# Four of the later token tiles normalised on GpSimd instead of VectorE, in the prologue of an adaLN block

## The chip, the cores and the metric

The kernel runs on one core of one Trainium2 chip. The core's engines work side by side, each through its own list of instructions in order: TensorE (PE in the profile, with its weight loads as PEld), VectorE (DVE), ScalarE (ACT), GpSimd (POOL) and SyncE (SP), which issues nearly all DMAs. They wait for each other through semaphores. The metric is the time of one execution on the device in microseconds (us), as the median of several runs. The span of a profiled execution is from its first to its last instruction.

## The reference

One transformer block whose two halves are modulated by a condition vector `c`. There are 2048 tokens of width 1024, 32 query heads of width 32 that share one key and one value head, and a gated feed-forward part of width 3584. Everything is stored as bf16.

```python
mod = (silu(c) @ w_mod).reshape(1, 6, 1, 1024)
sa, ca, ga, sb, cb, gb = mod[:, 0], ..., mod[:, 5]
h = layernorm(x) * (1 + ca) + sa
q = (h @ wq) split into 32 heads of 32;  k = h @ wk;  v = h @ wv
o = softmax(q k^T / sqrt(32)) v          # k and v are shared by all heads
x = x + ga * (o @ wo)
h = layernorm(x) * (1 + cb) + sb
x = x + gb * ((silu(h @ w1) * (h @ w3)) @ w2)
```

## The kernel before

**Tiling.** Tokens come in 16 tiles of 128. A tile lies in `X` with tokens on partitions. It is normalised there, written to a scratch tile (`XN` and other regions that are free at that time), transposed by TensorE in 128x128 pieces and stored in `HT`, with channels on partitions. Keys `KT` (four copies, one for each quarter of the partitions), values `V` and queries `QT` are projected from `HT`. Attention runs over 8 blocks of 256 queries. In a block, the heads come in 8 groups `f` of four. A step of attention (function `step`) takes one group and 256 keys: eight score matmuls (line 915) into two of three pairs of PSUM banks, then two exponentials on ScalarE (line 925). A whole block has 64 steps, and the kernel 512, with 1024 exponentials. Sums of exponentials on VectorE (lines 942 to 957), products with `V` (line 975) and with a selection matrix for the softmax denominators (line 1002) follow, and their results are taken from PSUM by VectorE (lines 1011 to 1028). After each block, `post` adds the output projection (line 1107), normalises again and computes the feed-forward part (lines 1141 and 1175), while the next block's exponentials run.

**Prologue.** Before the first scores, the scale and shift of the first modulation are computed from `w_mod`, the first eight token tiles are normalised and transposed, and the keys of the first 1024 tokens are projected. The scale is folded into the weights, the shift into biases (function `bias`; its matmuls are on line 758). The first block treats the groups f = 0 to 3 specially: it first takes all four over the first half of the keys, then all four over the second half. So the exponentials begin while tiles 8 to 15 are still to be normalised, transposed and turned into keys and values. The norm of a tile has these steps, in functions `ln`, `ln_stats`, `ln_scale` and `ln_norm`:

- two statistics instructions on VectorE (line 530) and one that joins them (line 532);
- on GpSimd, adding epsilon (line 551) and the power -0.5 (line 553), which give the reciprocal standard deviation `RS`;
- one `tensor_scalar` over 128x1024 elements (line 573), which subtracts the mean and multiplies by `RS`. It runs on the engine that `en` names, here VectorE for all 16 tiles. Tiles 2 and 5 have their statistics on ScalarE.

Four normalised tiles are transposed together (function `tr`, matmuls on line 587) in four groups of eight matmuls, two channel chunks each; VectorE takes tiles 8 to 15 out of PSUM (line 601, two instructions for each group).

**PSUM banks.** There are eight. During attention six belong to the scores. What else TensorE does in the prologue from 29 us on goes through the two others, `PB[0]` and `PB[1]`: the bias products, the projections of keys, values and queries (lines 637, 648 and 658), the transposes of tiles 8 to 15, and the products of line 975 and 1002. A bank is free when its result has been taken out.

**The order of the work.** No engine's list is written out by hand. `Dag.add` collects the instructions with what they read and write, an engine, a priority (smaller is earlier) and a cost in us; `Dag.schedule` plays the execution through with these costs and fixes for each engine the order in which it will run; `Dag.emit` writes the lists and the semaphores. The costs only set the order. The rules that matter here:

- TensorE takes a score step that is ready first. Then come transposes and key projections (priority 1) and the bias products (priority 0). Value and denominator products come before query projections (priority 5) while TensorE is in the mode of scores and value products, or when they have been ready for more than 1 us; otherwise after them.
- A group of matmuls that opens a bank is placed only when a bank is free. Query, key and value projections open their banks in the order of the program: q of f=2, q of f=3, then the keys of the second half.
- VectorE takes the smallest priority, and of equal ones the earlier in the program; what has been ready for more than 4 us is raised by 3. Evictions have 1 or less, statistics and norms 2.
- GpSimd takes norms (priority 2) before the small steps of the reciprocal standard deviation (priority 5).

The cost of a norm in this planning is in `ln_norm`:

```python
writes=[("XN", q)] + xnk(q), dur=0.42 if en == "dve" else 1.2, prio=2 - bp)
```

The prologue's token tiles go through

```python
def ln(t):
    (ln_stats_act if t in ONACT else ln_stats)(t)
    ln_scale(t, 1)
    ln_norm(t, t, en="pool" if t in ONPOOL else "dve")
```

The norms inside `post` call `ln_norm` without `en` and run on VectorE.

Of the kernel before, what the change touches and what calls it, by code (L numbers as in the profile page):

```python
# [380 lines left out]
def build(nc, x_in, wq_in, wk_in, wv_in, wo_in, w1_in, w3_in, w2_in, c_in, wmod_in, out, S, D, F):  # L381
# [167 lines left out]
    def ln_scale(t0, n):  # L549
        rk = [("RS", t0 + i) for i in range(n)]  # L550
        G.add("pool", lambda e: e.tensor_scalar(RS[:, t0:t0 + n], MV[:, t0:t0 + n, 1], EPS, None, ALU.add),
              reads=[("MV", t0 + i) for i in range(n)], writes=rk, dur=0.3)
        G.add("pool", lambda e: e.tensor_tensor(RS[:, t0:t0 + n], RS[:, t0:t0 + n], NHALF[:, 0:n], ALU.pow),
              reads=rk + ["NHALF"], writes=rk, dur=0.4)
# [16 lines left out]
    def ln_norm(t, q, s=None, bp=0, en="dve"):  # L571
        s = t % NXS if s is None else s
        G.add(en, lambda e: e.tensor_scalar(xnt(q), X[:, s, :], MV[:, t, 0:1], RS[:, t:t + 1],
                                               ALU.subtract, ALU.mult),
              reads=[("X", s), ("RS", t), ("MV", t)], writes=[("XN", q)] + xnk(q), dur=0.42 if en == "dve" else 1.2, prio=2 - bp)
# [90 lines left out]
        return [("QT", f, q0 + i) for i in range(0, qn, P)]  # L666

    ONACT = (2, 5)
    ONPOOL = ()
    KP = 1  # L670
    QACT = 1
    TRP = 1
# [5 lines left out]
# [5 lines that stand above are left out]
# [549 lines left out]
def bass_adaLN_cond__grouped_kv_mqa__glu_gated_swiglu__prompt_kernel(nc, A_x, A_wq, A_wk, A_wv, A_wo, B_x, B_w1, B_w3, B_w2, c, w_mod, out):  # L1232
    _, S, D = [int(v) for v in A_x.shape]
    F = int(B_w1.shape[1])
    build(nc, A_x, A_wq, A_wk, A_wv, A_wo, B_w1, B_w3, B_w2, c, w_mod, out, S=S, D=D, F=F)
# [28 lines left out]
```

## Time and profile before

| what | us |
|---|---|
| median of 3 runs (1159.92 to 1161.35) | 1159.93 |
| the profiled execution, its whole time | 1159.92 |
| its span | 1158.1 |
| busy: TensorE, ScalarE, VectorE, GpSimd | 1122.6, 1027.6, 984.7, 43.5 |
| 1024 exponentials on ScalarE (line 925) | 968.6 |
| norms of tiles 8 to 15 on VectorE, mean of one | 0.53 to 0.54 |
| ScalarE idle between 30 and 62 us, four waits before exponentials (2.56, 0.76, 1.29, 5.57) | 10.2 |

The mean granted clock of TensorE was 0.990. How to read the rows: a row of the timeline has the start, the length of the stretch, engine, line, operation, what it writes and reads with the shape, and how many instructions were joined (`x8`); in brackets stand the idle time of the engine before it and what ended it. A row of a group has the busy time of all its instructions and the mean of one in ns. `WREG`, `GSB`, `GBB` and `UREG` as outputs of line 573 are scratch for normalised tiles: 8 to 13 go to `WREG`, 14 to `GSB`, 15 to `GBB`. The six banks of the scores are called `SP` in the rows and the other two `PB`.

### The profile page before, as it was taken

The numbers are of one execution on the slowest core, as the hardware profiler recorded it, in microseconds if no ns is written. First come the engines' busy times: TensorE is split into PE (matmuls) and PEld (weight loads), VectorE is DVE, ScalarE is ACT, GpSimd is POOL, SyncE is SP. The second block draws the span as 40 slices with busy tenths as digits, with TensorE's granted clock in tenths as the row PEclk, the third lists the DMA queues.
The fourth block names the chain that finished last, engine by engine and source line by source line (L and its number), as shares of the span: only waits on it lengthen the run. The fifth ranks groups of instructions, "written<-read, shape, count | busy, mean of one in ns | idle before, by whom it ended". The sixth has DMA issues, their size and how long they took to land.

```text
span 1158.1 us, 35702 instructions
## 1 busy us (share of the span) xinstructions
PE 1122.6 (97%) x15918; PEld 767.1 (66%) x15918; DVE 984.7 (85%) x1498; ACT 1027.6 (89%) x1170; POOL 43.5 (4%) x86
## 2 busy tenths in 40 slices
PE   7799998999979999999999999999999999999998
PEld 6564444776646766777577766776677766777887
DVE  5837889999888999899999998999989999997452
ACT  5789999999999999999999999999999999992110
POOL 3200001000000001000100001000100010000000
PEclk8899999999989999999999999999999999999999
DMA  9337005956546565856496567766586649756996
GB/s 331 113 129 220 19 2 127 275 169 178 166 122 190 169 193 149 248 170 192 119 279 196 159 177 194 226 169 174 152 252 181 185 122 258 204 152 192 284 291 160
DMA packets 385417, 211.10 MB, mean 182 GB/s; under 512 B 21744, under 2 KB 376048, under 8 KB 385264
## 3 DMA queue, kind: packets, MB, share of 16 engines
q1 hardware_dynamic: 383184, 208.69, 64.5%
q8 instruction: 125, 2.05, 0.8%
q10 hardware_dynamic: 2080, 0.13, 0.1%
q14 instruction: 28, 0.23, 0.1%
HBM read 201.46 MB, written 4.19 MB: 178 GB/s over the span
## 4 chain that ended last, share of the span: by engine, by line
PE 92%; ACT 3%; DVE 3%; DMA 1%; SPq 1%; issue 0%; POOL 0%; DVEq 0%
PE PB L1141 33%; PE PB L1175 16%; PE SP L915 14%; PE PB L975 11%; PE PB L1107 5%; PE PB L658 4%; PE SP L1141 3%; ACT UREG L925 3%; PE SP L1175 2%; PE PB L1002 2%; DMA UREG<-in_w_mod_dram 1%; PE PB L637 1%; PE PB L838 0%; PE SP L1107 0%; DVE WO L850 0%
## 5 line engine op out<-in xcount | busy, mean ns | idle before, releaser
L925 ACT ACTIVATE UREG<-SP 128x1024 bf16<-128x1024 f32 x1024 | 968.6, 1075 | 18.8 <-PE SP L915 16.4
L948 DVE TENSOR_TENSOR UREG<-UREG 128x2048 bf16<-128x2048 bf16 x240 | 292.8, 1220 | 12.8 <-ACT UREG L925 10.8
L915 PE MATMUL SP<-QT,KT 32*128 32x256 bf16 x4096 | 204.8, 274 | 16.0 <-ACT UREG L925 15.0
L1141 PE MATMUL PB<-QT,WREG 128*128 128x256 bf16 x1648 | 207.4, 274 | 1.8 <-DVE DSB L1026 1.6
L1141 PEld LDWEIGHTS PB<-QT,WREG 128*128 128x128 bf16 x1648 | 150.1, 98 | 46.8 <-issue 31.2
L942 DVE TENSOR_TENSOR UREG<-UREG 128x2048 bf16<-128x2048 bf16 x120 | 146.4, 1220 | 11.5 <-PE PB L1002 6.4
L915 PEld LDWEIGHTS SP<-QT,KT 32*128 32x128 bf16 x4096 | 61.2, 93 | 138.6 <-ACT UREG L925 79.6
L1141 PE MATMUL PB<-QT,HREG 128*128 128x256 bf16 x1056 | 133.7, 274 | 0.8 <-DVE DSB L1026 0.8
L975 PE MATMUL PB<-UREG,V 128*32 128x256 bf16 x4032 | 132.2, 277 | 1.7 <-DVE QT L610 0.9
L975 PEld LDWEIGHTS PB<-UREG,V 128*32 128x32 bf16 x4032 | 99.3, 98 | 27.5 <-issue 17.9
L1141 PEld LDWEIGHTS PB<-QT,HREG 128*128 128x128 bf16 x1056 | 96.1, 98 | 29.7 <-issue 19.6
L1175 PE MATMUL PB<-WREG,HREG 128*128 128x256 bf16 x812 | 101.2, 273 | 0.0
L1175 PEld LDWEIGHTS PB<-WREG,HREG 128*128 128x128 bf16 x812 | 75.3, 98 | 20.4 <-issue 11.4
L1175 PE MATMUL PB<-HREG 128*128 128x256 bf16 x532 | 67.8, 274 | 0.0
L1141 PE MATMUL PB<-QT,X 128*128 128x256 bf16 x528 | 67.8, 274 | 0.0
L658 PE MATMUL PB<-HREG,WREG 128*128 128x512 bf16 (+1 forms) x312 | 64.1, 343 | 0.3 <-DVE DSB L1026 0.3
L957 DVE TENSOR_TENSOR UREG<-UREG 128x2048 bf16<-128x2048 bf16 x52 | 63.4, 1220 | 0.5
L1150 ACT ACTIVATE GSB<-GSB 128x512 bf16<-128x512 bf16 x56 | 38.8, 693 | 27.5 <-DVE GSB L1148 27.5
L1014 DVE COPY XN<-PB 128x256 f32<-128x256 f32 x63 | 26.6, 422 | 39.6 <-PE PB L1002 39.3
L1175 PEld LDWEIGHTS PB<-HREG 128*128 128x128 bf16 x532 | 49.2, 98 | 14.3 <-issue 8.0
L1107 PE MATMUL PB<-WO,QT 128*128 128x512 bf16 x232 | 57.6, 381 | 0.2 <-DVE QT L661 0.2
L1141 PEld LDWEIGHTS PB<-QT,X 128*128 128x128 bf16 x528 | 48.2, 98 | 14.3 <-issue 9.3
(139 smaller groups left out, 1031.9 us busy)
## 6 DMA issues: line engine op xcount, KB each, us to landing
WREG<-in_B_w_dram SPq DMA_DIRECT2D x112, 512.0 KB, 5.1
HREG<-in_B_w_dram SPq DMA_DIRECT2D x74, 512.0 KB, 5.2
WREG<-in_B_w_dram SPq DMA_DIRECT2D x33, 896.0 KB, 5.1
X<-in_B_w_dram SPq DMA_DIRECT2D x38, 512.0 KB, 5.1
HREG<-in_B_w_dram SPq DMA_DIRECT2D x21, 896.0 KB, 5.2
X<-in_B_w_dram SPq DMA_DIRECT2D x10, 896.0 KB, 5.1
X<-in_A_x_dram SPq DMA_DIRECT2D x32, 256.0 KB, 5.0
WREG<-in_w_mod_dram SPq DMA_DIRECT2D x16, 512.0 KB, 4.7
```

The lines of the kernel that those rows point to most:

```text
L658: g = mm_group(NC, lambda e, b, c: e.matmul(b[:, 0:n], WQ[:, c, f * P:(f + 1) * P], HT[:, c, sl], start=c == 0, stop=c == NC - 1), lambda ...
L915: r = e.matmul(SP[:, b, o:o + qn], KT[32 * gg:32 * gg + 32, kts[j] * P:(kts[j] + 1) * P], QT[32 * gg:32 * gg + 32, f, q0:q0 + qn], start=T ...
L925: G.add("act", lambda e, u=u, h0=h0, n=n, b0=b0, nb=nb: e.activation(U[:, u, h0 * W:(h0 + n) * W].rearrange("p (b w) -> p b w", b=nb), SP[ ...
L942: G.add("dve", lambda e, tr=tr, u=u, fu=first_u: e.tensor_tensor(TR[:, tr, 0:4 * W], U[:, fu, 0:4 * W], U[:, u, 0:4 * W], ALU.add), reads= ...
L948: G.add("dve", lambda e, tr=tr, u=u: e.tensor_tensor(TR[:, tr, 0:4 * W], TR[:, tr, 0:4 * W], U[:, u, 0:4 * W], ALU.add), reads=[("TR", tr) ...
L957: G.add("dve", lambda e, ta=ta, tb=tb: e.tensor_tensor(TR[:, ta, 0:4 * W], TR[:, ta, 0:4 * W], TR[:, tb, 0:4 * W], ALU.add), reads=[("TR", ...
L975: r = e.matmul(PB[g.bank][32 * gg:32 * gg + 32, 0:qn], V[:, kt, :], U[:, pu, (gg * npk + j) * qn:(gg * npk + j + 1) * qn], start=w0 + n == ...
L1014: G.add("dve", lambda e, g=g, f=f: e.tensor_copy(ASB[:, f % 4, 0:qn], PB[g.bank][:, 0:qn]), writes=[("ASB", f % 4), ("XN", 2 + f % 4 // 2) ...
L1107: g = mm_group(NC, lambda e, b, f, t=t, h=h: e.matmul(b, QT[:, f, t * P:(t + 1) * P], WO[:, f, h * 512:(h + 1) * 512], start=f == 0, stop= ...
L1141: return e.matmul(b[:, j * qn:(j + 1) * qn], w13[:, w, c, j * P:(j + 1) * P], QT[:, c, q0:q0 + qn], start=c == 0, stop=c == NC - 1)
L1150: G.add("act", lambda e, b=b: e.activation(TB[b], GS[b], ACT.Tanh, scale=0.5), reads=[("GS", b)], writes=[("TB", b)], clear=alias("TB") if ...
L1175: G.add("pe", lambda e, g=g, j=j, fc=fc, hf=hf, first=first, w2s=w2s: e.matmul(PB[g.bank][:, j * 256:(j + 1) * 256], HHT[:, hf * NH + fc, ...
```

## The change

The tuple that names the token tiles whose norm runs on GpSimd was empty and now holds four tiles.

```diff
     ONACT = (2, 5)
-    ONPOOL = ()
+    ONPOOL = (9, 11, 13, 15)
     KP = 1
```

For tiles 9, 11, 13 and 15, `ln` now calls `ln_norm` with `en="pool"`: the same `tensor_scalar` of 128x1024 elements, with the same operands, is put on GpSimd's list, with a planning cost of 1.2 in place of 0.42. The statistics of these tiles stay on VectorE, and tiles 8, 10, 12 and 14 are normalised on VectorE as before. As every list comes from the planner, the order of other instructions can change too.

## The prediction

> **What bounds the kernel now.** I read the table of busy time by stage first, then ScalarE's, TensorE's and VectorE's instructions in order of time between 26 and 62 us, then GpSimd's rows. Columns of the stage table: length, busy us of TensorE (PE), its weight loads (PEld), VectorE (DVE), ScalarE (ACT) and GpSimd (POOL), each with a count, then the granted clock and DMA.
>
> ```profile
> core 0: us, PE busy (x) PEld busy (x) DVE busy (x) ACT busy (x) POOL busy (x), PEclk, DMA share, GB/s
> 35.00:47.00 12.00, 9.79 (x217) 6.28 (x216) 10.31 (x27) 9.38 (x10) 4.08 (x10) 0.72 0.33 90
> 47.00:62.00 15.00, 12.16 (x262) 8.62 (x265) 11.99 (x36) 9.41 (x11) 0.99 (x2) 1.00 0.44 121
> 62.00:90.00 28.00, 27.68 (x523) 18.69 (x516) 10.07 (x22) 27.42 (x30) 0.00 (x0) 1.00 0.31 108
> 400.00:600.00 200.00, 199.19 (x2864) 134.64 (x2861) 185.06 (x273) 198.98 (x224) 6.86 (x8) 1.00 0.68 188
> 1100.00:1158.00 58.00, 53.70 (x492) 47.84 (x490) 22.69 (x35) 5.66 (x9) 0.00 (x0) 1.00 0.90 226
> ```
>
> From 62 us ScalarE and TensorE are both full (27.4 and 27.7 of 28; 199.0 and 199.2 of 200), and after the last exponential (1047 us) TensorE alone works off the rest. So time is still to be had where both stand idle, at the start, and what ScalarE gains before 62 us should reach the end. The norms that the change moves run from 34.9 to 51.3 us, in two stages in which PE lacks 2.2 and 2.8 us and ACT 2.6 and 5.6 us.
>
> ```profile
> 35.60 7.44 ACT L925 ACTIVATE UREG<-SP 128x1024 bf16<-128x1024 f32 x8 [2.56 <-PE SP L915]
> 43.80 1.94 ACT L925 ACTIVATE UREG<-SP 128x1024 bf16<-128x1024 f32 x2 [0.76 <-PE SP L915]
> 47.02 9.27 ACT L925 ACTIVATE UREG<-SP 128x1024 bf16<-128x1024 f32 x10 [1.29 <-PE SP L915]
> 61.86 19.00 ACT L925 ACTIVATE UREG<-SP 128x1024 bf16<-128x1024 f32 x20 [5.57 <-PE SP L915]
> ```
>
> In brackets is the idle time before a row. The four waits of the exponentials are the region's cost. The longest, 5.57 us, is for the first scores of head group f=3, whose queries are projected only after all transposes:
>
> ```profile
> 40.90 1.00 PE L758 MATMUL PB<-SAB,WO 128*128 128x1 bf16 x32
> 48.52 1.07 PE L587 MATMUL PB<-IDENT,WREG 128*128 128x128 bf16 x16
> 55.40 0.40 PE L587 MATMUL PB<-IDENT,WREG 128*128 128x128 bf16 x4 [0.40 <-DVE HREG L601]
> 59.67 1.05 PE L658 MATMUL PB<-HREG,WREG 128*128 128x256 bf16 x8
> 61.41 0.40 PE L915 MATMUL SP<-QT,KT 32*128 32x256 bf16 x8
> ```
>
> Transposes (48.5 to 55.9), two value and denominator products (56.1 to 59.7), the projection, then the scores: one line through the two free PSUM banks PB0 and PB1, emptied by VectorE.
>
> **The change part by part.**
>
> *VectorE.* Four norms leave it. Each takes 0.534 us, 0.46 from start to start, so 1.8 us in all; those of tiles 9, 11 and 13 (39.95, 42.80, 44.56) stand in a gapless stretch, that of 15 (50.73) amid the transposes' evictions. No DMA is added; X slots 1, 3, 5 and 7 are handed on by GpSimd instead, and the loads behind them (35.5 on) are first needed after 170 us: nothing.
>
> *GpSimd.* The trace has no such instruction. Nearest rows:
>
> ```profile
> L521 POOL COPY QT<-SCT 128x512 bf16<-128x512 bf16 x2 | 1.2, 611 | 4.1 <-DVE SCT L518 4.1
> ```
>
> ```profile
> 185.60 1.08 POOL L551 TENSOR_SCALAR RS<-MV 128x1 f32<-128x1 f32 x1 [135.42 <-DVE MV L532]
> 186.77 0.57 POOL L553 TENSOR_TENSOR RS<-RS,NHALF 128x1 f32<-128x1 f32 x1
> ```
>
> Half the columns take 0.61, so 0.61 is the lower end and 1.22 the doubled row. The same L551 takes 0.21 where VectorE is in its statistics and 1.08 here, beside a 1.17 us VectorE add that ends with it: GpSimd was held. Two such holds of 0.9 give 3.0, the upper end. I take 1.22, plus 0.3 for one hold. What stands behind each on GpSimd is the rstd pair (0.22 + 0.57) of the next tiles, and VectorE waits for those in order.
>
> On this the Trainium skill (SBUF — State Buffer, Who interferes with whom) speaks against the change: one port pair is shared, a VectorE tensor_scalar in its fast mode and any GpSimd instruction exclude each other, and whichever comes second is blocked for the whole of the other. The row agrees for GpSimd as the one held; no row shows VectorE held. By the rule each moved norm could cost VectorE a whole GpSimd norm where one of its own falls on it, an estimated 4 x 1.2 = 4.8 us, and the sum would turn from 2.4 us gained to 2.4 lost.
>
> I add no such loss: beside the places that I work out for the four norms below, VectorE's list has statistics and PSUM evictions, and one norm.
>
> *Order.* The list is planned with 1.2 us for a GpSimd norm (0.42 on VectorE). I worked the planner's rules through from 39.95; they decide order, the times are this trace's.
> 1. Without tile 9's norm the two v evictions (L651) start 0.45 earlier, bank PB1 frees, and the bias product L758, which stood behind the score step of 40.34, is put before it. At half clock (0.50 granted from 39.0 to 45.6) it runs 40.3 to 41.25. The scores land at 41.8 instead of 40.95: new wait of ScalarE, 41.9 - 41.17 = 0.7.
> 2. TensorE is now in score mode when PB0 frees, and in that mode the planner takes the value and denominator products of f=0 (1.83 + 1.74 at half clock) before q of f=2. They end at 45.3, the next scores at 45.7: ScalarE waits from 43.75, 2.0, where it waited 0.76 + 1.29.
> 3. By then tiles 8 to 11 are normalised (tile 11 on GpSimd: 42.6 to 43.8), so the transposes go next: TensorE 45.8 to 49.35, set by evictions at 0.36 and the norms of 12 and 14. VectorE reaches tile 15's last statistics only at 49.6, so when a bank frees there the second four aren't ready, and q of f=2 goes in at 49.6. Evicted at 51.15, it gives scores at 51.7: ScalarE, done at 49.5, waits 2.4.
> 4. Norm 15 on GpSimd: 49.65 + 0.85 (rstd) + 1.2 = 51.7; TensorE comes for it at 52.6. The second transposes run under the eight exponentials of f=2 (51.85 + 8 x 0.927 = 59.3), and so does q of f=3, evicted at 57.4. It is wanted at 58.35. The wait of 5.57 goes.
> 5. Late next are the second half's keys: at 61.2 by this order, first needed after f=3 at 66.7.
>
> Sum: away 0.76 + 1.29 + 5.57 = 7.62; new 0.7 + 2.0 + 2.4 = 5.1; gain 2.5 us. ScalarE enters the full stretch at 59.3 instead of 61.86. TensorE then stands 0.4 us of products behind where it stood; it has 2.6 us of idle from 90 to 120 and 12.5 from 120 to 400 to take them. I keep 2.4.
>
> The profiled execution took 1159.92 us, span 1158.1 and 1.8 around it, as the median 1159.93. Predicted: 1159.9 - 2.4 = 1157.5.
>
> *A longer norm.* With duration p, tile 15 is ready at max(49.65, 44.5 + 2p) + 0.85 + p. TensorE is late from p = 2.1, ScalarE (0.95 in hand) from 2.7; at 3.0 the gain shrinks to 1.6 (54.35 - 52.6 - 0.95 = 0.8 lost), and at 3.5 it is gone. Below 1.22 nothing is gained, as VectorE's queue, not GpSimd, brings tile 15's statistics.
>
> **The rivals.** 0.2%, or 2.3 us, is about what a measurement of this kernel can tell from no change.
>
> *A shorter queue, same order.* The transposes stay behind the scores of f=2. Then VectorE's 0.6 us of statistics at 47.04 leaves the path to q of f=2, and 0.46 goes between evictions; the transposes end 1.1 sooner and so do q and scores of f=3: 1158.8. For it: ScalarE's stretch from 47.02 is full and sets those score steps. Against: the bias product's weights are issued at 23.4 and land within 10.5, by 33.9, so that it lacks only the bank.
>
> *Slower: both queries behind all eight transposes.* If tile 15 is normalised before the bank frees at 49.6, the transposes keep both banks to 52.5; then value products to 54.3, q of f=2 at 55.3, scores at 55.9. ScalarE waits 7.0 from 49.5, the two groups end at 56.4 + 14.8 = 71.2 instead of 61.86 + 7.4 = 69.3: 1.9 later, 1161.8, and up to 2 more if so long a gap halves the granted clock again, as it was after the thin stretch before 39 us. It decides if tile 15 is normalised 2.1 us sooner than I have it; its aggregate stands behind six evictions and two norms on VectorE, which the planner's priorities put first.
>
> *More.* TensorE's later idle shrinks too, since the keys of the second half and value products are done sooner against the scores: up to 1.5 of the 2.6 us from 90 to 120, so 1156.0.
>
> *GpSimd is slow.* At p = 4.5 tile 15 is ready at 58.85, 6.2 late, and scores of f=3 come 2.7 later than now: 1162.6. The rows speak against it: it needs more than three holds for each norm.
>
> That the norms stay on VectorE is excluded: ln passes the engine by tile, and all four tiles go through it.
>
> **How the numbers follow.** My forecast 0.48 (own range 1156.4 to 1158.8), more 0.15, same order 0.17, slower by order or clock 0.15, slow GpSimd 0.05. The forecast lies on the bound, so 0.29 of its 0.48 count as faster. Faster: 0.29 + 0.15 + 0.02 of the shorter queue = 0.46; slower: 0.12 of the order's 0.15 and the 0.05 = 0.17; the rest, 0.37, within 0.2%. The order is replanned to the end of the kernel, where I followed it only to 62 us; ScalarE is idle some 8 us from there to 1047, so little can be won and some lost. Range 1154.8 to 1162.3.
>
> **What would show it.** The bias product ahead of a score step near 40 us; transposes of tiles 8 to 11 at about 46 instead of 48.5; q of f=2 between the two sets of transposes; scores of f=3 right behind those of f=2, with no wait over 3 us on ScalarE after 50 us; GpSimd norms of 1.2 to 1.5 us; VectorE norms that stay at 0.53. Wrong if the norms take over 2.6 us, if VectorE is held, if the granted clock halves between 47 and 56, or if ScalarE's waits after 62 us grow by what was won.

## The result and the profile after

The changed kernel takes 1166.41 us (median of 4 runs, 1164.16 to 1167.61) against 1159.93 us. The ratio is 1.0051, with a 95% interval of 1.0033 to 1.0070: slower by 4 to 8 us, where 2.4 us less was predicted and the range ended at 1162.3. The profiled execution took 1167.1 us, with a span of 1165.3 us. TensorE's time in that span went from 1122.6 us busy and 35.5 idle to 1125.4 busy and 39.9 idle; more idle time and slower matmuls both count.

The table of busy time by stage, changed kernel, with the columns of the table shown before:

```profile
core 0: us, PE busy (x) PEld busy (x) DVE busy (x) ACT busy (x) POOL busy (x), PEclk, DMA share, GB/s
35.00:47.00 12.00, 9.66 (x210) 6.42 (x208) 11.03 (x26) 8.68 (x10) 10.24 (x10) 0.72 0.25 68
47.00:62.00 15.00, 8.48 (x108) 5.74 (x112) 7.56 (x22) 8.67 (x10) 9.72 (x7) 0.68 0.33 88
62.00:90.00 28.00, 27.57 (x570) 18.63 (x566) 11.61 (x28) 24.08 (x26) 0.00 (x0) 0.99 0.41 134
110.00:116.00 6.00, 4.60 (x60) 1.97 (x57) 6.00 (x15) 5.16 (x7) 0.00 (x0) 0.82 0.93 284
52.40:62.60 10.20, 5.54 (x64) 4.00 (x68) 5.45 (x16) 4.17 (x6) 4.41 (x2) 0.50 0.38 103
```

The stage from 47 to 62 us carries the damage. TensorE is busy for 8.5 of its 15 us, where it had 12.2, the granted clock is 0.68 instead of 1.00 (0.50 from 52.4 to 62.6 us), and GpSimd, which had 1 us of work there, has 9.7. From 110 to 116 us the clock is 0.82, where before it was 1.00. GpSimd's instructions in order of time show what fills it:

```profile
35.54 3.81 POOL L573 TENSOR_SCALAR WREG<-X,MV,RS 128x1024 bf16<-128x1024 bf16 x1 [2.10 <-DVE WREG L573]
...
43.17 3.80 POOL L573 TENSOR_SCALAR WREG<-X,MV,RS 128x1024 bf16<-128x1024 bf16 x1
46.93 0.56 POOL L553 TENSOR_TENSOR RS<-RS,NHALF 128x1 f32<-128x1 f32 x1
47.47 0.22 POOL L551 TENSOR_SCALAR RS<-MV 128x1 f32<-128x1 f32 x1
47.68 3.80 POOL L573 TENSOR_SCALAR WREG<-X,MV,RS 128x1024 bf16<-128x1024 bf16 x1
51.45 0.55 POOL L553 TENSOR_TENSOR RS<-RS,NHALF 128x1 f32<-128x1 f32 x1
...
53.11 3.80 POOL L573 TENSOR_SCALAR GBB<-X,MV,RS 128x1024 bf16<-128x1024 bf16 x1
```

A norm on GpSimd takes 3.80 us, seven times VectorE's 0.54. The small steps of the reciprocal standard deviations (551 and 553) stand between the norms: the second step of tile 14 waits from 47.69 until norm 13 has ended, and tile 15's own pair comes after that. So tile 15 is ready at 56.91. TensorE in that stretch:

```profile
45.74 1.05 PE L658 MATMUL PB<-HREG,WREG 128*128 128x256 bf16 x8
...
51.01 0.40 PE L915 MATMUL SP<-QT,KT 32*128 32x256 bf16 x8 [0.66 <-ACT UREG L925]
57.06 0.58 PE L587 MATMUL PB<-IDENT,WREG 128*128 128x128 bf16 x4 [5.65 <-POOL GBB L573]
...
58.85 0.61 PE L915 MATMUL SP<-QT,KT 32*128 32x256 bf16 x8
...
61.88 1.39 PE L975 MATMUL PB<-UREG,V 128*32 128x256 bf16 x32
...
64.07 1.05 PE L658 MATMUL PB<-HREG,WREG 128*128 128x256 bf16 x8
```

It waits 5.65 us for norm 15. Behind that wait, in the order of the list, stand not only the transposes of tiles 12 to 15 but a score step of f=2 (58.85), then the value and denominator products, and the queries of f=3 (64.07). The exponentials show this as two waits:

```profile
41.91 1.94 ACT L925 ACTIVATE UREG<-SP 128x1024 bf16<-128x1024 f32 x2 [0.76 <-PE SP L915]
45.86 1.94 ACT L925 ACTIVATE UREG<-SP 128x1024 bf16<-128x1024 f32 x2 [2.01 <-PE SP L915]
48.10 5.61 ACT L925 ACTIVATE UREG<-SP 128x1024 bf16<-128x1024 f32 x6 [0.30 <-PE SP L915]
59.52 1.94 ACT L925 ACTIVATE UREG<-SP 128x1024 bf16<-128x1024 f32 x2 [5.81 <-PE SP L915]
...
66.26 3.89 ACT L925 ACTIVATE UREG<-SP 128x1024 bf16<-128x1024 f32 x4 [2.65 <-PE SP L915]
```

ScalarE waits 5.81 us in the middle of f=2 and 2.65 before f=3, which starts at 66.26 instead of 61.86: 4.4 us later. From the starts of the later exponentials in both traces, 1.1 us is added by 79 us and 2.8 between 104 and 124 us, 1.3 of it comes back, and from 352 us to the last exponential the distance is constant at 7.2 us, which is also that of the spans (1165.3 - 1158.1).

### The profile page after: what moved, and what is told of

It is laid out like the page before. It is cut to its first block, busy times and chain, and to the rows that moved or that the text cites. A ratio compares the mean times of both kernels' runs of the same rounds, so it can differ in the third digit from the quotient of the medians.

```text
span 1165.3 us, 35683 instructions
## 1 busy us (share of the span) xinstructions
PE 1125.4 (97%) x15908; PEld 766.6 (66%) x15908; DVE 985.1 (85%) x1494; ACT 1028.4 (88%) x1170; POOL 58.3 (5%) x90
## 4 chain that ended last, share of the span: by engine, by line
PE 91%; DVE 3%; ACT 2%; POOL 1%; DMA 1%; SPq 1%; issue 1%; DVEq 0%
PE PB L1141 33%; PE PB L1175 16%; PE SP L915 14%; PE PB L975 10%; PE PB L658 5%; PE PB L1107 4%; PE SP L1141 3%; PE SP L1175 2%; PE PB L1002 2%; ACT UREG L925 2%; SPq L695 1%; DMA UREG<-in_w_mod_dram 1%; DVE ST L530 1%; PE PB L637 1%; PE PB L838 0%
## 5 line engine op out<-in xcount | busy, mean ns | idle before, releaser
L551 POOL TENSOR_SCALAR RS<-MV 128x1 f32<-128x1 f32 x32 | 19.3, 609 | 1008.4 <-DVE MV L532 1008.3
```

## The experiments

Two theories stood at the outset. A: the length of the GpSimd norms is the cause, through what stands behind them on GpSimd and TensorE, and the new order by itself gains. B: the new order of the lists is the cause, whatever engine runs the norms. Ratios below are to the kernel before, run on the same chip beside each kernel.

**Short norms in the new order.** GpSimd's norms treat 320 of the 1024 columns; the rest is set to zero, once, at the start.

```diff
-        G.add(en, lambda e: e.tensor_scalar(xnt(q), X[:, s, :], MV[:, t, 0:1], RS[:, t:t + 1],
+        w = D if en == "dve" else SHORT
+        G.add(en, lambda e: e.tensor_scalar(xnt(q)[:, 0:w], X[:, s, 0:w], MV[:, t, 0:1], RS[:, t:t + 1],
```

> The changed kernel, every list in the same order, but the four GpSimd norms take only the first 320 of their 1024 columns (the other 704 are set to zero at the start and stay zero, so these four tiles are not normalised in full). By 3.80 us for 1024 columns a norm should last about 1.2 us, which is what the planning charged. Theory A, the length of the GpSimd norm is the whole loss: the 5.65 us in which TensorE waited for the norm of tile 15 goes, the first exponentials of f=3 start at 66.3 - 5.8 - 0.3 = 60.2 or earlier, ahead of the 61.9 of before, and the time is 1157.5 to 1159. Theory B, the new order itself loses: the start of f=3 improves likewise, but the 3.5 us that the changed kernel lost after it (exponentials 4.4 us late at f=3, 7.9 us late at step 48) are lost again, and the time is 1161 to 1163. Theory C, sharing between GpSimd and VectorE: VectorE norms beside a GpSimd norm stay above 1 us and f=3 starts no earlier than 61.9.

Measured: 1159.32 us, 0.3 above A's range and well below B's; ratio 0.9991 (0.9980 to 1.0002). A norm took 1.45 us, close to the 1.52 that the prediction had assumed, and the exponentials of f=3 started at 58.35, so C falls too. (1.2 us of this lead over the kernel before is there already at 34.4 us, before any of the moved norms was needed.) So the loss goes away with the length of the norm. With the length that I had assumed, the kernel comes out about 1 us ahead, which this measurement can't tell from nothing, and not 2.4.

**The other two corners.** In the new order, the four norms are put back on VectorE's list, at their planned times; in the old order, they are put on GpSimd's list in the same way. The edit for the first, after the planner has run:

```diff
+    for n in norms:
+        G.order[n.eng].remove(n)
+        n.eng = "dve"
+        o = G.order[n.eng]
+        o.insert(next((i for i, m in enumerate(o) if m.start > n.start), len(o)), n)
```

> The changed kernel with its planned order on TensorE, ScalarE and the DMA queue, but the four norms put back on VectorE's list, at the places where the plan had them start on GpSimd. It tells the order from the engine. Theory A (only the length on GpSimd costs): each norm costs VectorE 0.46 us, first exponentials of f=3 at 60 to 61, time 1157.5 to 1159.5. Theory B (the order loses by itself): 1161 to 1163. If both the norms' length and the order cost, it lies between.

> The kernel before with its planned order everywhere, but the four norms of tiles 9, 11, 13 and 15 put on GpSimd's list at their planned places. It tells the engine from the order. Theory A: GpSimd has 4 x 3.8 us of norms with the reciprocal deviations of the next tiles behind each; tile 14's comes at about 52.4, VectorE stands at its norm until then with the evictions of the transposes behind it, tile 15 is ready at about 57.5, where the transposes wanted it at 52.1, so the first exponentials of f=3 come 5.5 late, at 67.4, and the time is 1164 to 1167. Theory B: the loss is in the replanned order, and with the old order the time stays below 1162.

Measured: new order on VectorE 1159.21 us, ratio 0.9988 (0.9979 to 0.9997); old order on GpSimd 1167.95 us, ratio 1.0064 (1.0050 to 1.0078), a little above what A gave. With the two kernels of the case this is a complete table of ratios:

| | norms on VectorE | norms on GpSimd |
|---|---|---|
| old order | 1 | 1.0064 |
| new order | 0.9988 | 1.0051 |

Moving the norms costs 0.63 to 0.64%, 7.3 us, in either order. The new order gains 0.12%, 1.4 us, with VectorE's norms, where the interval ends just below 1; with GpSimd's norms it is 0.13%, but there the intervals of the two ratios overlap. B falls. ScalarE in the new order with VectorE's norms:

```profile
42.48 1.94 ACT L929 ACTIVATE UREG<-SP 128x1024 bf16<-128x1024 f32 x2 [0.95 <-PE SP L919]
45.76 11.11 ACT L929 ACTIVATE UREG<-SP 128x1024 bf16<-128x1024 f32 x12 [1.34 <-PE SP L919]
58.76 3.89 ACT L929 ACTIVATE UREG<-SP 128x1024 bf16<-128x1024 f32 x4 [1.90 <-PE SP L919]
```

f=3 starts 3.1 us earlier than in the kernel before. In the profiled execution 1.2 us of this went by 71 us, where value products and keys stand between scores, and another 2.7 between 97 and 117 us, of which 1.4 came back; at the end 0.5 us was left. In the median it was 1.4.

**Why a norm takes 3.8 us.** GpSimd instructions are added near the end of the kernel before, on 128x1024 elements that nothing reads afterwards; then two norms on GpSimd beside norms, adds and statistics on VectorE. Only the lengths of the instructions are read from this run.

```diff
+        fns = [lambda e: e.tensor_copy(dst(0), src),
+               lambda e: e.tensor_scalar(dst(1), src, m, r, ALU.subtract, ALU.mult),
+               lambda e: e.tensor_scalar(dst(2)[:, 0:512], src[:, 0:512], m, r, ALU.subtract, ALU.mult),
+               lambda e: e.tensor_scalar(dst(3), src, r, None, ALU.mult),
+               lambda e: e.tensor_scalar(dst(4), src, 0.5, 2.0, ALU.subtract, ALU.mult),
+               lambda e: e.tensor_tensor(dst(5), src, UREG[:, 1024:2048], ALU.mult)]
```

> The kernel before with extra instructions at its end, whose results nobody uses: on GpSimd one after the other a copy of 128x1024 bf16, the norm's tensor_scalar with two per-partition operands over 1024 and over 512 columns, one with a single per-partition operand, one with two constants, and a tensor_tensor; then two norms beside fast tensor_scalars of VectorE. If GpSimd's time goes by columns alone, the copy takes 1.2 us (0.61 for 512 before) and the norm as much. If the length comes with the operation, the norm takes 3.8 and its half 1.9 to 2.0; if it is the per-partition operands, the one with constants takes 1.2. VectorE's tensor_scalar takes 0.54 alone; if GpSimd shuts it out for a whole instruction, one takes up to 4.3 beside a norm, if it only holds it for a while, about 1.4 as the norm of tile 12 did.

GpSimd's instructions in order of time:

```profile
1068.87 1.04 POOL L1218 COPY UREG<-UREG 128x1024 bf16<-128x1024 bf16 x1
1069.90 3.97 POOL L1219 TENSOR_SCALAR UREG<-UREG,MV,RS 128x1024 bf16<-128x1024 bf16 x1
1073.87 2.09 POOL L1220 TENSOR_SCALAR UREG<-UREG,MV,RS 128x512 bf16<-128x512 bf16 x1
1075.94 2.85 POOL L1221 TENSOR_SCALAR UREG<-UREG,RS 128x1024 bf16<-128x1024 bf16 x1
1078.86 3.64 POOL L1222 TENSOR_SCALAR UREG<-UREG 128x1024 bf16<-128x1024 bf16 x1
1082.46 2.12 POOL L1223 TENSOR_TENSOR UREG<-UREG 128x1024 bf16<-128x1024 bf16 x1
```

The copy takes 1.04 us, near the 1.22 that the prediction had for the norm. The norm takes 3.97, and about half of it on half the columns (2.09). With constants in place of the per-partition operands it is 3.64, so these operands account for 0.33 us; with one operation and one operand it is 2.85. Most of the price comes with the operation. A product of two tensors takes 2.12, less than any of them on 1024 columns; why `tensor_scalar` is slower than that no run shows.

What a GpSimd norm does to VectorE stands in the summary of VectorE's norms of this run (minimum, median, maximum in ns), and in two of them:

```profile
L1235 DVE TENSOR_SCALAR UREG<-UREG,MV,RS x6: 534/544/1333, 1155.2 to 1160.1; 128x1024 bf16<-128x1024 bf16 x6
1155.65 1.33 DVE L1235 TENSOR_SCALAR UREG<-UREG,MV,RS 128x1024 bf16<-128x1024 bf16 x1
1160.08 0.82 DVE L1235 TENSOR_SCALAR UREG<-UREG,MV,RS 128x1024 bf16<-128x1024 bf16 x1
```

The one that began 0.37 us after the first GpSimd norm (1155.28) took 1.33 us. One that began 0.79 us after the second norm (1159.29) took 0.82. The four others took 0.53 to 0.55: one began just ahead of the first norm, three later under it. The holds are 0.8 and 0.3 us, not the 4 us of the norm.

**A plan that knows the length.** Both kernels are planned anew, with the measured cost; the second moves two norms only.

```diff
-              ... dur=0.42 if en == "dve" else 1.2, prio=2 - bp)
+              ... dur=0.42 if en == "dve" else 3.8, prio=2 - bp)
```

> The changed kernel with one number of the plan altered: a norm of GpSimd is planned at 3.8 us instead of 1.2, so that the order of every engine is made for the length that was measured. The instructions are the same. In the new order the queries of f=2 and f=3 both stand ahead of the second set of transposes on TensorE, so only the second half of the keys waits for tile 15. Theory A (the damage is the order made for 1.2 us while the norms take 3.8, with work queued behind the transposes): the f=3 exponentials no longer wait for tile 15, the 5.81 us wait before them falls below 2 us, and the time falls to 1159 to 1162. Theory B (the four norms on GpSimd cost their length wherever they are planned, since the second half of the keys waits for tile 15 next): a wait of 3 us or more returns at the first step that uses the second half, and the time stays at 1164 to 1168.

> Two norms only on GpSimd, those of tiles 9 and 11, planned at 3.8 us; 13 and 15 go back to VectorE. Theory A (length of the GpSimd norms and what they hold up at the end of the chain of the tiles): GpSimd is through with both by about 43 to 45 us, the rstd pairs of tiles 13 to 15 are not held, tile 15 is ready at 50 to 51 as before, and the time is that of the kernel before or up to 2 us less, 1157.5 to 1160. Theory B (any 3.8 us norm among the prologue's work costs about its length): two norms cost half of what four did, 1162 to 1164.

Measured: four norms 1163.18 us, ratio 1.0022 (1.0012 to 1.0032), between the two theories; two norms (`ONPOOL = (9, 11)`) 1159.14 us, as A had it, ratio 1.0000 (0.9991 to 1.0008). ScalarE with four norms planned at 3.8:

```profile
46.39 11.12 ACT L925 ACTIVATE UREG<-SP 128x1024 bf16<-128x1024 f32 x12 [1.87 <-PE SP L915]
57.96 1.94 ACT L925 ACTIVATE UREG<-SP 128x1024 bf16<-128x1024 f32 x2 [0.45 <-PE SP L915]
```

The planner puts the queries of both groups ahead of the transposes of tiles 12 to 15, and the waits of 5.81 and 2.65 us are gone; f=3 starts at 57.96, 3.9 us before the kernel before. That part of theory A holds. But the span is 3.2 us longer than the kernel before's. With two norms the same contrast is larger: f=3 starts 5.8 us earlier and the last exponential 5.5 us earlier, yet the span is only 1.7 shorter, and in the medians nothing is left. The planner lays out the whole kernel, so a change at 45 us also re-sorts work hundreds of us later. The stage from 400 to 700 us and the end, with four norms planned at 3.8:

```profile
400.00:700.00 300.00, 294.62 (x4222) 199.12 (x4220) 276.58 (x402) 297.94 (x337) 5.66 (x10) 0.99 0.65 179
1040.00:1161.00 121.00, 116.86 (x1121) 100.05 (x1120) 62.34 (x107) 18.56 (x28) 1.58 (x4) 1.00 0.88 230
```

and in the kernel before:

```profile
400.00:700.00 300.00, 298.79 (x4269) 202.08 (x4267) 279.31 (x409) 298.86 (x338) 8.59 (x10) 1.00 0.67 184
1040.00:1158.00 118.00, 113.69 (x1095) 97.41 (x1092) 60.73 (x105) 18.64 (x28) 1.69 (x4) 1.00 0.87 228
```

TensorE loses 4.2 us between 400 and 700 us and has 3.2 us more left from 1040 us on, while ScalarE is as far at 1040 us as before. What is left after the last exponential tells the same: 114.1 us with four and with two norms planned at 3.8, and 110.2 in the kernel before. With two norms TensorE is busy for 1122.6 us in all, as before, and idle for 33.8 instead of 35.5. So a head start of ScalarE that TensorE doesn't use is only work left over for the end. I didn't follow which instructions of the plan caused the 4.2 us.

**One norm at a time, in the new order.** Only tile 15's norm back on VectorE; only tile 15's on GpSimd; only tile 9's on GpSimd. Each is the edit of the lists shown above, with another set of tiles.

> The changed kernel in its own order on every engine, but the norm of tile 15 stands in VectorE's list at its planned place; 9, 11 and 13 stay on GpSimd. Theory A (each norm of 3.80 us holds the rstd pairs behind it, and tile 15 is the last link): the pair of tile 15 still waits for norm 13, which ended at 51.5, its norm then takes 0.55 on VectorE instead of 3.80, tile 15 is ready at 53.4 to 53.8 instead of 56.9, the f=3 exponentials start 3.3 us earlier, at about 63, and the time is 1162.5 to 1164. Theory B (what is lost is lost on VectorE, which is held while GpSimd runs its norms): it changes by less than 1 us, 1165.5 to 1167.

> The changed kernel in its own order on every engine, but the norms of tiles 9, 11 and 13 stand in VectorE's list; only tile 15 stays on GpSimd. Theory A: nothing long stands ahead of the rstd pair of tile 15, which is ready at 48 to 49, the norm ends at 52 to 53, about where the plan wants it for the second transposes, so f=3's exponentials start at 59 to 60.5 and the time is 1158.5 to 1160.5: one norm of 3.8 us costs next to nothing where four cost 7. Theory B (length of tile 15's own norm is what counts, since its transposes wait for it): a wait of 3 us stays before f=3, and the time is 1162 to 1165.

> The changed kernel in its own order, with the norms of tiles 11, 13 and 15 in VectorE's list; only tile 9 stays on GpSimd. Its norm runs from 35.5 to 39.3 in the changed kernel, its transposes stand at 46 to 47, and no rstd pair stands behind it before 41. Theory A (a GpSimd norm costs only what it delays, through the pairs behind it and the transposes of its tile): nothing is delayed, VectorE is 0.5 us lighter, f=3's exponentials start at 58 to 59, and the time is that of the same order with all norms on VectorE, 1158.5 to 1159.5. Theory B (each 3.8 us norm costs about a quarter of the 7.5 us that four cost): 1160.5 to 1161.5.

Measured: 1163.79 us, ratio 1.0030 (1.0018 to 1.0042); 1162.04 us, ratio 1.0019 (1.0008 to 1.0029); 1158.95 us, ratio 0.9989 (0.9981 to 0.9998). Against the 0.9988 of the same order without a GpSimd norm, the norms of 9, 11 and 13 cost 4.9 us, that of 15 alone 3.6, all four 7.3, and that of 9 nothing that intervals of 1 us either way can show. The first is in A's range, with f=3 at 63.65. For tile 15 alone theory A had 1158.5 to 1160.5: a miss, with the median at the lower end of B's range. The third is in A's range, with f=3 at 59.65, a little later than expected. GpSimd and TensorE of the second kernel, with tile 15's norm alone on GpSimd:

```profile
49.30 3.94 POOL L573 TENSOR_SCALAR GBB<-X,MV,RS 128x1024 bf16<-128x1024 bf16 x1
```

```profile
53.39 0.38 PE L588 MATMUL PB<-IDENT,WREG 128*128 128x128 bf16 x4 [1.66 <-POOL GBB L573]
```

Nothing long stood ahead of tile 15's pair, and still the norm ended at 53.24, 1.66 us after TensorE came for it: I had called that "about where the plan wants it". What a GpSimd norm costs is what waits for it: nothing for tile 9, whose transposes come more than 7 us after its norm has ended, and 3 to 4 us for the last tile of all.

**The clock after 98 us.** In the six profiled executions of the new order with long, short or VectorE's norms a part of the gain was lost between 98 and 130 us, where the granted clock fell, and just before it TensorE waited 1.0 to 1.4 us for the eviction of line 1026 (1030 or 1032 in the edited kernels), which VectorE does behind a reciprocal. The two are swapped, in the new order with all norms on VectorE, and with tile 9's on GpSimd.

```diff
+        if a in recips[0:2] and b in evicts:
+            b.start, o[i], o[i + 1] = a.start, b, a
```

> The new order with all norms on VectorE, as in the run before of that kind (ratio 0.9988 to the kernel before), and one swap on VectorE: the eviction of the denominators (L1026) that TensorE waits for 1.36 us at 104 us goes ahead of the second reciprocal instead of behind it. Five profiled runs of this order show that wait (1.1 to 1.4 us), and in each the granted clock falls to 0.5 to 0.8 in the 3 us after it; three profiled runs of other orders show neither. Theory A (the wait brings the drop of the clock, and the drop costs the 2 us that were lost between 98 and 125 us): the wait falls to about 0.5 us, the clock stays at 1.00 there, and the time falls 1 to 2 us below that order's, to 1157 to 1158.5. Theory B (the clock falls for another reason): the wait falls, the clock falls all the same, and the time is 0.3 to 0.9 us below, 1158.3 to 1159.

> Tile 9 alone on GpSimd in the changed kernel's order, and the swap of the eviction L1026 with the second reciprocal. If both theories A of the two runs beside it hold, the gains add: 1156.5 to 1158.5, the shortest of all. If the clock falls all the same: 1158 to 1159.5.

Measured: 1159.37 us, ratio 0.9990 (0.9981 to 0.9998), and 1158.91 us, ratio 0.9987 (0.9978 to 0.9996). TensorE and the stages in the first of them:

```profile
104.73 0.60 PE L659 MATMUL PB<-HREG,WREG 128*128 128x512 bf16 x2 [0.22 <-DVE DSB L1030]
```

```profile
110.00:113.00 3.00, 2.07 (x35) 1.10 (x35) 2.84 (x6) 2.96 (x4) 0.00 (x0) 0.82 0.92 298
113.00:116.00 3.00, 3.00 (x19) 0.87 (x15) 1.68 (x4) 2.56 (x3) 0.00 (x0) 0.61 0.81 255
```

The wait shrank from 1.36 to 0.22 us, the clock fell all the same, some 6 us later (0.82, 0.61), and the time did not move. With tile 9's norm on GpSimd the wait shrank from 1.01 to 0.56 us, and the clock was 0.50 from 107 to 113 us in both kernels. So this wait isn't what decides the clock, or not alone: in the first kernel other waits of 0.84 and 0.93 us came in its place, and the kernel with two norms planned at 3.8 shows a wait of 1.33 us at 107.7 with the clock at 1.00. The expectation also overlooked the old order with GpSimd's norms, whose clock falls to 0.55 with no wait over 0.6 us in the 20 us before. Nor does TensorE's busy time around the wait separate them. Three stretches, of the new order with VectorE's norms, of the two norms planned at 3.8, and of the old order with GpSimd's norms:

```profile
102.70:105.70 3.00, 1.60 (x26) 0.61 (x23) 3.00 (x8) 2.16 (x3) 0.00 (x0) 1.00 0.79 251
104.80:107.80 3.00, 1.63 (x17) 0.51 (x16) 3.00 (x6) 3.00 (x5) 0.00 (x0) 1.00 1.00 343
116.00:119.00 3.00, 3.00 (x21) 0.90 (x21) 1.11 (x2) 2.36 (x4) 0.00 (x0) 0.55 1.01 353
```

A count over the thirteen traces does separate them. The granted clock changes in steps of 3.41 us. Leave out the matmuls of a single column (line 865, products of the condition vector with `w_mod`): then TensorE was busy for at most 0.52 of each of the 34 steps at whose end the clock fell, and for at least 0.53 of each of the 4084 other steps at full clock, from 45 us to near the end. With these matmuls counted the two overlap: up to 0.78 before a fall, down to 0.53 elsewhere. This was found after the runs, and none was made to test it.

The fastest kernels of the study are the four in the new order with at most tile 9 on GpSimd. Their ratios, 0.9987 to 0.9990, can't be told from each other. They are some 1.3 us faster than the kernel before, which each interval, ending just below 1, only just supports.

## Why the prediction was wrong, by its own steps

*GpSimd.* This step failed. It took 1.52 us for a norm, 1.22 of it from a copy row doubled for the columns, with 3.0 as the upper end, from two holds. The norm takes 3.80 us, well past the 2.6 us that the text named as a sign of being wrong. The doubling was sound (a copy of 1024 columns takes 1.04), but a `tensor_scalar` isn't a copy, and no row of the trace before had GpSimd arithmetic on a wide tile; with that gap the upper end should not have been built from holds alone. GpSimd's one-column instructions, which the trace had, show nothing of the rate for each element. The Trainium skill has one-input operations of GpSimd at "roughly line-rate" (GPSIMD Engine Reference, Engine selection); here the copy, at 1.04 us for 1024 columns, doesn't contradict that, and the norm, which has one tensor input too, is at 3.80.

*A longer norm.* The formula for tile 15 was right: at 3.8 it gives 52.1 + 0.85 + 3.8 = 56.75, and 56.91 was measured. The price was not. By the step's own lines, 56.75 is 4.15 late for TensorE and 3.2 for ScalarE, so 1160.7. The changed kernel took 1166.4. It left out what is queued behind the waiting transposes: the next score step of f=2, and behind it the products and the queries of f=3. It had a halved clock only as a sign of being wrong, not in the price: the clock was granted at 0.50 from 52.4 to 62.6 us, and the first four transposes after the wait take 0.58 us, where four took 0.40 before. So f=3 started at 66.26, and not at 59.3 + 3.2 = 62.5; no run separates the two shares. After that 2.8 us more were lost that the step had at nothing.

*Order.* Points 1 and 2 came as foretold: new waits of 0.76 and 2.01 us for 0.7 and 2.0. Point 3 was wrong in the kernel's favour: the queries of f=2 went in at 45.74, ahead of the transposes, so that ScalarE waited 0.30 us there and not 2.4. Point 4 was wrong the other way: the queries of f=3 stayed behind the second set of transposes and the value products, so that even with VectorE's norms 1.90 of the 5.57 us remain. That the two nearly cancel is luck: f=3 at 59.3 by the sum, 58.76 in the run with VectorE's norms and 58.35 with short ones. Point 5, the keys, was harmless in the sum and cost 1.1 us before 79 us, since keys and products stand between scores.

*VectorE.* Nearly right. (The first norm that moves begins at 39.95; what stands at 34.9 is tile 8's.) Its norms stayed at 0.53 to 0.55 us, except that of tile 12, which began beside a GpSimd norm, and two scalings of weights (line 744) took 0.58 and 0.63 instead of 0.35:

```profile
43.20 1.43 DVE L573 TENSOR_SCALAR WREG<-X,MV,RS 128x1024 bf16<-128x1024 bf16 x1
...
48.43 0.58 DVE L744 TENSOR_SCALAR WREG<-WO,MODC 128x512 bf16<-128x512 bf16 x1
...
52.03 0.55 DVE L573 TENSOR_SCALAR GSB<-X,MV,RS 128x1024 bf16<-128x1024 bf16 x1 [2.36 <-POOL RS L553]
```

The prediction quoted a rule of the Trainium skill (SBUF — State Buffer, Who interferes with whom) by which the engine that comes second is blocked for the whole instruction of the other. For this pair it is too strict: the three holds are of 0.2 to 0.9 us, beside GpSimd norms of 3.80. What cost VectorE more is the last row: its norm of tile 14 waited 2.36 us for a reciprocal standard deviation that stood behind a GpSimd norm. The prediction named that queue but didn't price it.

*What ScalarE gains before 62 us should reach the end.* This step failed as well. It held among kernels of the new order: f=3 is 7.5 us later with GpSimd's norms than with VectorE's, and the span 7.7 longer. It did not hold between orders, where a gain was to come from: with VectorE's norms in the new order, 3.1 us at f=3 were 0.5 in the span and 1.4 in the median, and with two norms planned at 3.8, 5.8 us were 1.7 and nothing.

*The chances.* What came true was the rival "GpSimd is slow", with a chance of 0.05 and a price of 1162.6 at 4.5 us. Both were too small, for the reasons above. The range ended at 1162.3, 4.1 below the result.

## What to carry to other kernels

Price an instruction on another engine from the same operation on that engine, and where the trace has none, let the upper end of the range be several times the nearest row. A late instruction costs what stands behind it in the lists of its own engine and of the one that waits for it, and not only its lateness; the last link of a chain pays in full, an early one with slack pays nothing. Where two engines are both full, count the idle time of the one that works to the end: what the other gains counts only as far as that idle time shrinks.

## What was not expected of the hardware

- GpSimd on 128x1024 bf16: copy 1.04 us, product of two tensors 2.12, `tensor_scalar` with one operation 2.85, with two 3.64 to 4.08. So `tensor_scalar` is slower there than an operation with two tensors. VectorE's two-operation `tensor_scalar` takes 0.54.
- A VectorE `tensor_scalar` from SBUF that begins within 0.8 us after the start of a GpSimd one of 1024 columns is through 1.3 to 1.7 us after that start, as if it were let go 0.9 to 1.2 us after it. With 320 columns on GpSimd (42.00, 1.45 us) it was 0.3 us: VectorE's norm from 42.03 took 0.85. Later ones under the same GpSimd instruction run at their usual 0.53 to 0.54, and copies from PSUM (line 601) that begin right after a GpSimd norm (47.75 and 53.16) take their usual 0.42.
- In the thirteen traces, from 45 us on, the granted clock fell only at the end of steps of 3.41 us in which TensorE was busy for at most 0.52 without its single-column matmuls, and stayed in all steps with 0.53 or more; time that is busy with single-column matmuls did not keep it up.
